# The eighth quad of batch 3's first MLP product as seven half-size products, with a new order at both ends of its chains

## The chip, the cores and the metric

One core of a Trainium2 chip. The metric is the device time of one execution in microseconds (us): the median over runs, lower is better. The kernel before takes 297.79 us (three runs, 297.66 to 298.02). The engines are named as in the profile: PE is TensorE (matmuls; PEld its weight loads), DVE is VectorE, ACT is ScalarE, POOL is GpSimd, SP is SyncE, which here only starts transfers.

## The reference

Block-sparse attention over 4 batches of 768 tokens, then a residual MLP block:

```
attn = softmax(where(mask, q @ k.T / 8, -1e9)) ; x = (attn @ v)      # 4 x 768 x 512
a1 = alpha1 * x + beta1
u  = x + lam * (w_tok @ a1)                                          # over tokens
a2 = alpha2 * u + beta2
h  = maximum(a2 @ w_ch1, 0)                                          # 512 -> 2048
out = u + lam * (h @ w_ch2)                                          # 2048 -> 512
```

The change touches only the last batch (number 3): its first MLP product `a2 @ w_ch1` and the order in which the second, `h @ w_ch2`, begins.

## The kernel before

**Order.** The kernel is emitted by hand-written strings of tokens: each letter takes the next job from a queue, and each engine works its own instructions strictly in the order of emission. `WEAVE` joins the strings; the last four, `W3`, drive the end of batch 3 when no other batch has work left. In them `f` is a job of the first MLP product, `g` one of the second, `S` a VectorE subtraction that prepares the second, `W` and `D` VectorE sums of weights and of activations that prepare the first. The other letters belong to earlier work.

**First stage.** The hidden layer has 2048 rows in 16 blocks of 128; the 768 tokens are two halves c = 0, 1 of 384. Blocks n and n + 8 (`HN` is 8) at both halves form *quad n*: four results of 128 x 384 each. Directly a quad takes four matmuls for each result, 16 in all, each 128 x 128 weights against 384 columns (`job_f1`, matmul at L920, relu by ScalarE at L927). Quads 0 to 6 (`FS` is 7) are computed instead as a 2 x 2 block product with seven half-size products (Strassen's scheme in Winograd's form), two matmuls each, 14 in all (`job_m`, matmul at L1028). Their operands include sums of weight blocks (`job_w`, L978, tile `wsum`) and of activation blocks (`job_d`, L993). Quad 7 was direct.

Within a quad the products 1, 6, 5, 3 accumulate in one bank of the PSUM memory, in this order. After 1, 6 and 5 ScalarE copies the partial sum out (`keep_sum`, L1003, tile `part`), and the next product of the chain may only write once that copy has been read; after 3 ScalarE's relu (L1039) writes the first result. Product 2 has a bank of its own, products 7 and 4 share another; VectorE adds the kept sums to them (L1044) and a relu follows one addition later (`relu_late`, L1011). Product 4 accumulates on the bank of 7 after 7's addition has read it. `last_f1` interleaves the quads: product m of quad n stands in slot 7 n + k, with k = 0, 4, 6, 8, 10, 12, 16 for m = 1, 6, 2, 5, 7, 3, 4. The four direct results of quad 7 stand in slots 1 and 5 (beginning) and 49 and 55 (end).

**Banks.** PSUM gives two `sp` tiles (chains of quads with n % 3 below 2, and chains of the second stage), three `mm` tiles (products 2 and 7, and the like of the second stage) and one `op` tile (chains of quads with n % 3 = 2). A new tile waits until the one that had its place has been read.

**Second stage.** The same scheme: for a pair of token tiles t and t + 3 (t = 0, 1, 2) seven products of eight matmuls with 256 columns each (`job_p` calls `mul`, matmul at L1184), whose results VectorE adds to `x_sb` (`plus`, L1194). Product 1 of tile t needs the first eight hidden blocks at c = 0, so the results of (n,3) for all quads. VectorE forms four differences a tile first (`job_s`, L1157: S1 writes X1, S2 X2, S3 and S4 overwrite parts of `hts`); product 6 needs X2, 7 needs S3, 5 X1, 3 S4. They can be done in halves: `R1` for quads 0 to 3, `R2` for 4 to 7, `ALL` for both. `P_ORDER` and `S_ORDER` hold the order of products and differences. Finished rows are stored by SP and, at the very end, by ScalarE's queue (`emit_store`, L1083).

Of the kernel before, what the change touches and what calls it, by code (L numbers as in the profile page):

```python
# [18 lines left out]
B = 4  # L19
H = 8  # L20
S = 768
D = 64
# [3 lines left out]
DM = 512  # L26
P = 128
# [53 lines left out]
]  # L81
W3 = [
# [4 lines left out]
]  # L87
STR = (2, 3)
HN = NH // 2
HC = DM // 2  # L90
FS = 7
FW = 6
WEAVE = W1 + W2 + W2L + W3
ENG = {
    "kT0": 0,
# [154 lines left out]
def kernel(  # L250
# [211 lines left out]
    def sp_tile():  # L462
        return psum.tile([P, 2, 512], FP, name="sp", tag="sp", bufs=2)
# [6 lines left out]
    def mm_tile(shape=(P, DM), dt=FP):  # L470
        return psum.tile(list(shape), dt, name="mm", tag="mm", bufs=3)

    def op_tile(shape):
        phase["op"] += 1
        if phase["first"] and phase["op"] % 2 == 0:
            return mm_tile(shape)
        return psum.tile(shape, FP, name="op", tag="op", bufs=1)
# [246 lines left out]
    rest = ptile([P, P], FP, "rest")  # L724
# [225 lines left out]
        7: (3, 3),  # L950
    }

    def w_of(name, ks, n):
        if isinstance(name, int):
            at = n.start // FW
            return wsum[at][:, name - 1, ks, (n.start - FW * at) * P : (n.stop - FW * at) * P]
        r, c = int(name[0]) - 1, int(name[1]) - 1
        at = slice((HN * r + n.start) * P, (HN * r + n.stop) * P)
        return w1b[:, 2 * c + ks.start : 2 * c + ks.stop, at]
# [6 lines left out]
        return uTs[B - 1][:, 2 * r + ks.start : 2 * r + ks.stop, ts(1 - c, QC)]  # L966

    def job_w(n, ks, cs):
        at = cs.start // FW
        if len(wsum) == at:  # L970
            tag, bufs = (("x_sb", 3), ("xs", 4))[at]
            shape = [P, 4, 2, (cs.stop - cs.start) * P]
            wsum.append(ap_.tile(shape, BF, name="wsum", tag=tag, bufs=bufs))
        a, b, op = WSUM[n]
        for name in (a, b):
            for k in range(ks.start, ks.stop):
                assert isinstance(name, str) or ("W", name, k, at) in did
        nc.vector.tensor_tensor(  # L978
            out=w_of(n, ks, cs), in0=w_of(a, ks, cs), in1=w_of(b, ks, cs), op=op
        )  # L980
        did.update(("W", n, k, at) for k in range(ks.start, ks.stop))
# [32 lines left out]
    def job_m(n, m):  # L1014
        b = B - 1
        if m == 1 and n % 3 < 2:
            chain[(n, 1)] = sp_tile()[:, 0]
        elif m == 1:
            chain[(n, 1)] = op_tile([P, DM])[:]
        elif m in (2, 7):  # L1020
            chain[(n, m)] = mm_tile()[:]
        ps = chain[(n, {2: 2, 7: 7, 4: 7}.get(m, 1))]
        w, u = PROD1[m]
        for k in range(2):
            ks = slice(k, k + 1)
            assert isinstance(w, str) or ("W", w, k, n // FW) in did
            assert isinstance(u, str) or ("D", u, k) in did
            nc.tensor.matmul(  # L1028
                ps[:, 0:QC],
                w_of(w, ks, slice(n, n + 1))[:, 0],  # L1030
                u_of(u, ks)[:, 0],
                start=(m in (1, 2, 7) and k == 0),
                stop=(k == 1),
                skip_group_check=True,
            )
        if m in (1, 6, 5):
            keep_sum(n, m)
        elif m == 3:
            nc.scalar.activation(h_row(b, 0, n), ps[:, 0:QC], AF.Relu)  # L1039
            did.add(("f", b, 0, n))  # L1040
        else:
            part, c, row = {2: (1, 1, n), 7: (5, 0, HN + n), 4: (6, 1, HN + n)}[m]
            h = h_row(b, c, row)
            nc.vector.tensor_tensor(  # L1044
                out=h, in0=ps[:, 0:QC], in1=chain[(n, "s", part)][:], op=ALU.add
            )
            relu_late()
            raw.append((h, ("f", b, c, row)))

    def last_f1():  # L1050
        at = {1: 0, 6: 4, 2: 6, 5: 8, 7: 10, 3: 12, 4: 16}
        slot = {7 * n + k: (n, m) for n in range(FS) for m, k in at.items()}
        rest = [(c, r + n) for c in range(2) for n in range(FS, HN) for r in (0, HN)]
        jobs = []
        for k in range(max(slot) + 1):
            if k in slot:
                jobs.append(slot[k])
            elif rest and k in (1, 5, 49, 55):
                jobs.append((B - 1,) + rest.pop(0))
        return jobs + [(B - 1,) + j for j in rest]  # L1060

    chs = {}

# [106 lines left out]
    }  # L1170
    banks = {}

    def mul(b, t, n, ps, start, cols=slice(0, HC)):
        a, m, need = PROD[n]
        assert m in bq or all((m, r) in did for r in range(0, HN, 2))
        if need:
            assert all(("S", b, t, need, r) in did for r in range(HN))
        c, half = {"1": (0, 0), "X": (1, 0)}.get(a[0], (1, 0))
        if need == 0:
            h, half = divmod(int(a) - 11, 10)  # L1180
            assert all(("f", b, h, HN * half + r) in did for r in range(HN))
        rows = [r for r in range(HN) if r != FS - 1] + [FS - 1]
        for r in rows:
            nc.tensor.matmul(  # L1184
                ps,
                a_of(b, t, a)[:, r],
                b_rows(m, r)[:, 0, cols],
                start=(start and r == rows[0]),
                stop=(r == rows[-1]),
                skip_group_check=True,  # L1190
            )

# [5 lines left out]

    lo, hi = slice(0, HC), slice(HC, DM)

    def job_p(b, t, n):
        x = x_sbs[b]
        last = (b, t) == (B - 1, NT // 2 - 1)
        bk = banks.setdefault((b, t), {})
        if n in (1, 2, 7):
            bk[n] = sp_tile()[:, 0] if n == 1 else mm_tile()[:]
        if n == 3 and not last and 2 not in bk:
            bk[2] = mm_tile()[:]
        if n == 1:
            mul(b, t, 1, bk[1][:, lo], True)  # L1210
            plus(x[:, t, lo], bk[1][:, lo])
        elif n == 2:
            mul(b, t, 2, bk[2][:, lo], True)
            if last or b < B - 1:
                plus(x[:, t, lo], bk.pop(2)[:, lo])
            if last:
                emit_store(b, t, lo)
        elif n == 6:
            mul(b, t, 6, bk[1][:, lo], False)
            plus(x[:, t + 3, lo], bk[1][:, lo])  # L1220
        elif n == 7:
            mul(b, t, 7, bk[7][:, lo], True)
            plus(x[:, t + 3, hi], bk[7][:, lo])
        elif n == 5:
            mul(b, t, 5, bk[1][:, lo], False)
            plus(x[:, t : t + 4 : 3, hi], twice(bk[1][:, lo]))
        elif n == 4:
            mul(b, t, 4, bk[7][:, lo], False)
            plus(x[:, t + 3, lo], bk[7][:, lo])
            emit_store(b, t + 3, slice(0, DM))  # L1230
        elif last:
            for h in range(2):
                sl = slice(HC + h * P, HC + h * P + P)
                ps = (mm_tile(), op_tile([P, DM]))[h]
                mul(b, t, 3, ps[:, sl], True, ts(h, P))
                plus(x[:, t, sl], ps[:, sl])
                emit_store(b, t, sl, (nc.sync, nc.scalar)[h])
        else:
            sl = hi if b < B - 1 else slice(0, DM)
            mul(b, t, 3, bk[2][:, hi], b < B - 1)  # L1240
            plus(x[:, t, sl], bk[2][:, sl])
            emit_store(b, t, slice(0, DM))
        did.add((b, t, n))
# [36 lines left out]
    def start_mlp(b):  # L1280
# [8 lines left out]
        if b not in STR:  # L1289
# [2 lines left out]
            ]  # L1292
            return
        todo["g"] += [
            lambda j=j: job_p(b, *j) if len(j) == 2 else job_f2(b, *j[:2])
            for j in P_ORDER[b]
        ]
        todo["S"] += [lambda t=t, n=n, r=r: job_s(b, t, n, r) for t, n, r in S_ORDER[b]]
# [5 lines left out]
        + [(3, g, "g") for g in range(4)]  # L1304
        + [(t, 1) for t in (1, 2)]
        + [(t, n) for t in (1, 2) for n in REST],
        3: [(t, n) for n in (1, 2) for t in range(2)]
        + [(t, n) for t in range(2) for n in REST]
        + [(2, n) for n in (1, 2) + REST],
    }  # L1310
    ALL, R1, R2 = slice(0, HN), slice(0, HN // 2), slice(HN // 2, HN)
    S_ORDER = {
        2: [(t, n, ALL) for t in (1, 2) for n in (1, 2, 3, 4)],
        3: [(t, n, R1) for t in range(2) for n in (1, 2, 3)]
        + [(t, n, r) for t in range(2) for n, r in ((1, R2), (2, R2), (3, R2), (4, ALL))]
        + [(2, n, ALL) for n in (1, 2, 3, 4)],
    }

    def start_pair(i):
# [155 lines left out]
    def token(t, p):  # L1475
# [34 lines left out]
    both = slice(0, 2)  # L1510
    todo["W"] = [
        lambda n=n, k=k: job_w(n, k, slice(0, FW)) for n in (1, 3, 2, 4) for k in halves
    ] + [lambda n=n: job_w(n, both, slice(FW, FS)) for n in (1, 3, 2, 4)]
    todo["D"] = [lambda: job_d(1, both)] + [
        lambda n=n, k=k: job_d(n, k) for k in halves[::-1] for n in (2, 3, 4)
    ]
# [33 lines left out]
```

## Time and profile before

| | |
|---|---|
| median of three runs | 297.79 us (297.66 to 298.02) |
| profiled execution | 299.3 us, of which the span from first to last instruction 297.6 us |
| TensorE clock granted, mean | 0.999 |
| PE busy | 288.8 us |
| DVE busy | 239.1 us |
| ACT busy | 217.1 us |
| POOL busy | 110.0 us |
| first stage of batch 3 | from 256.58 us to about 276.4 us |
| second stage of batch 3 | from about 275.2 us to 294.1 us |

Times of rows are microseconds from the start of the span. A timeline row gives the start, the stretch covered, the engine, the line of the kernel, the operation, tile written and tiles read, their shapes, and how many instructions were merged (x2); in brackets the idle time ahead and what ended it. A TensorE row's stretch reaches to the modelled end of its last matmul, so consecutive rows overlap, and it is the distance from start to start that tells what a step costs the engine.

### The profile page before, as it was taken

How to read it: one execution, taken by the hardware profiler on the slowest of the kernel's cores; microseconds unless marked ns; L12 is line 12 of the kernel's file. 1: busy time of each engine (PE TensorE's matmuls, PEld its weight loads, DVE VectorE, ACT ScalarE, POOL GpSimd, SP SyncE). 2: the span in 40 equal slices, each digit the busy share in tenths (PEclk: the TensorE clock that was granted, in tenths of full speed). 3: DMA queues.
4: the chain of work that ended last, by engine and by line, in shares of the span. 5: the costliest groups of instructions: out<-in, count | busy, mean ns of one | idle time of the engine just before them, and what ended most of it. 6: DMA issues, size and time to landing. Idle time of an engine off the chain costs nothing.

```text
span 297.6 us, 7560 instructions
## 1 busy us (share of the span) xinstructions
PE 288.8 (97%) x3080; PEld 192.8 (65%) x3099; DVE 239.1 (80%) x492; ACT 217.1 (73%) x324; POOL 110.0 (37%) x149
## 2 busy tenths in 40 slices
PE   7999999999999999999999999999999999999995
PEld 2688878665467565565576566555567679765884
DVE  4988889995678887978768778795946999889994
ACT  5999989999798972999779690989869754577000
POOL 8997878632343720356322350335320300000000
PEclk9999999999999999999999999999999999999999
DMA  6999999971392996628853869743520211400032
GB/s 178 208 195 159 198 143 205 190 134 26 95 141 61 107 192 99 117 66 116 102 121 65 132 97 143 91 119 45 93 62 2 53 37 28 141 1 3 0 140 75
DMA packets 57275, 31.10 MB, mean 105 GB/s; under 512 B 37204, under 2 KB 54016, under 8 KB 57240
## 3 DMA queue, kind: packets, MB, share of 16 engines
q0 software_dynamic: 16752, 14.22, 33.4%
q1 hardware_dynamic: 40020, 15.92, 27.5%
q8 instruction: 24, 0.39, 0.6%
q10 hardware_dynamic: 468, 0.47, 0.5%
q14 instruction: 11, 0.09, 0.1%
HBM read 29.75 MB, written 6.29 MB: 121 GB/s over the span
## 4 chain that ended last, share of the span: by engine, by line
PE 82%; DMA 6%; DVE 6%; ACT 3%; POOL 1%; issue 1%; SPq 0%; POOLq 0%
PE mm L920 21%; PE mm L1070 14%; PE sp L602 8%; PE mm L847 8%; PE op L672 8%; PE mm L1184 5%; PE sp L1184 4%; DMA qpad<-in_q_dram 3%; PE mm L602 3%; PE mm L1028 2%; PE sp L1028 2%; ACT eT L620 2%; DMA uraw<-ubf 2%; PE op L649 2%; DVE eT L637 2%; PE mm L823 1%
## 5 line engine op out<-in xcount | busy, mean ns | idle before, releaser
L620 ACT ACTIVATE eT<-sp,expb 128x1024 f16<-128x1024 f32 x111 | 118.5, 1119 | 2.8 <-PE sp L602 2.2
L637 DVE TENSOR_TENSOR eT<-eT,mask 128x1024 f16<-128x1024 f16 x99 | 80.1, 835 | 14.2 <-ACT eT L620 14.0
L920 PE MATMUL mm<-uT,w1b 128*128 128x384 bf16 x400 | 73.9, 326 | 0.1
L706 POOL TENSOR_TENSOR a1pp<-x_sb,vbc 128x384 bf16<-128x384 f32 x25 | 28.5, 1140 | 120.5 <-DVE x_sb L690 85.9
L620 ACT ACTIVATE eT<-mm,expb 128x512 f16<-128x512 f32 x66 | 41.7, 685 | 26.5 <-PE mm L602 26.2
L927 ACT ACTIVATE hts<-mm 128x384 bf16<-128x384 f32 x100 | 47.1, 502 | 11.8 <-PE mm L920 11.1
L920 PEld LDWEIGHTS <-w1b 128*128 128x128 bf16 x400 | 37.2, 98 | 25.0 <-issue 2.6
L1070 PE MATMUL mm<-w2b,hts 128*128 128x512 bf16 x205 | 52.2, 379 | 0.9 <-issue 0.2
L672 PEld LDWEIGHTS <-eT 128*128 128x128 f16 x792 | 29.8, 98 | 9.2 <-issue 1.7
L1070 PEld LDWEIGHTS <-hts 128*128 128x128 bf16 x224 | 19.8, 98 | 22.3 <-issue 3.9
L672 PE MATMUL op<-vext,eT 128*128 128x65 f16 x792 | 32.1, 194 | 0.8 <-DVE x_sb L690 0.7
L602 PE MATMUL sp<-qTs,kTs 88*128 88x512 bf16 (+1 forms) x120 | 26.9, 325 | 1.4 <-ACT eT L620 0.7
L707 POOL TENSOR_TENSOR a1pp<-a1pp,vbc 128x384 bf16<-128x384 bf16 x25 | 26.7, 1070 | 2.0
L847 PE MATMUL mm<-a1pp,wtokT 128*128 128x256 bf16 x216 | 25.9, 273 | 0.1
L847 PEld LDWEIGHTS <-wtokT 128*128 128x128 bf16 x216 | 20.6, 98 | 5.6 <-issue 1.8
L1184 PEld LDWEIGHTS <-hts 128*128 128x128 bf16 x208 | 19.6, 98 | 3.0 <-issue 0.3
L859 DVE TENSOR_TENSOR x_sb<-x_sb,mm 128x512 f32<-128x512 f32 x18 | 12.3, 685 | 9.9 <-PE mm L847 9.8
L602 PE MATMUL sp<-qhT,khT 64*128 64x256 bf16 (+1 forms) x176 | 19.8, 322 | 0.0
L602 PEld LDWEIGHTS <-khT 64*128 64x128 bf16 x264 | 10.6, 94 | 12.7 <-issue 9.2
L649 PEld LDWEIGHTS <-eT 128*128 128x128 f16 x360 | 14.9, 97 | 3.8 <-issue 0.3
L1079 DVE TENSOR_TENSOR x_sb<-x_sb,mm 128x512 f32<-128x512 f32 x14 | 9.6, 685 | 8.8 <-PE mm L1070 6.7
L690 DVE TENSOR_TENSOR x_sb<-op,rcp 128x384 f32<-128x384 f32 x28 | 15.6, 557 | 1.0
(135 smaller groups left out, 384.9 us busy)
## 6 DMA issues: line engine op xcount, KB each, us to landing
out_dram<-x_sb SPq DMA_DIRECT2D x23, 256.0 KB
qpad<-in_q_dram POOLq DMA_DIRECT2D x15, 192.0 KB, 4.4
kr<-in_k_dram POOLq DMA_DIRECT2D x15, 192.0 KB, 5.4
vr<-in_v_dram POOLq DMA_DIRECT2D x15, 192.0 KB, 6.9
w1b<-in_moe_w_ch_dram POOLq DMA_DIRECT2D x4, 512.0 KB, 9.0
w2b<-in_moe_w_ch_dram POOLq DMA_DIRECT2D x4, 512.0 KB, 8.4
hts<-in_moe_w_tok_dram POOLq DMA_DIRECT2D x2, 576.0 KB, 8.3
x_sb<-in_k_dram ACTq DMA_DIRECT2D x2, 192.0 KB
```

The source lines that it names most:

```text
L602: nc.tensor.matmul(sp[jj][:, dst], lhsT, rhs, start=True, stop=True, skip_group_check=True,)
L620: nc.scalar.activation(dst, at, AF.Exp, bias=expb[:], scale=SCALE)
L637: nc.vector.tensor_mul(out=e, in0=e, in1=keep)
L649: nc.tensor.matmul(op[0][:, o, :], ets[u][:, jj, h * QB + n * P : h * QB + n * P + P], vexts[i % NVB][:, w, 2 * jp + jj, :], start=op[1] == 0,
L672: nc.tensor.matmul(op[0][:, o, :], ets[u][:, jj, h * QB + n * P : h * QB + n * P + P], vexts[i % NVB][:, w, 2 * jp + jj, :], start=op[1] == 0,
L706: eng.tensor_tensor(out=dst, in0=x_sbs[b][:, :, cols], in1=bc[0], op=ALU.mult)
L707: eng.tensor_tensor(out=dst, in0=dst, in1=bc[1], op=ALU.add)
L847: nc.tensor.matmul(ps[:, o], wtokT[:, os_, ts(2 * n + o, P)], a1pps[i][:, os_, :], start=(os_ == 0 and o == 0), stop=(os_ == NT - 1 and o ...
L920: nc.tensor.matmul(ps[:, 0:QC], w1b[:, dk, ts(n, P)], uTs[b][:, dk, ts(c, QC)], start=(dk == 0), stop=(dk == 3),)
L927: nc.scalar.activation(h_row(b, c, n), ps[:, 0:QC], AF.Relu)
L1070: nc.tensor.matmul(ps[:], ht[:, nk, ts(o % 3, P)], w2b[:, nk, :], start=(nk == 0), stop=(nk == NH - 1),)
L1184: nc.tensor.matmul(ps, a_of(b, t, a)[:, r], b_rows(m, r)[:, 0, cols], start=(start and r == rows[0]), stop=(r == rows[-1]), skip_group_che ...
```

## The change

Quad 7 goes the way of the others: `FS` and the direct slots disappear, and `job_m` covers all eight quads. Four weight sums for quad 7 are added (tile `wsum` of one block each for quads 6 and 7); the eight such sums no longer stand at the end of the first string of `W3`, but between the first `f` jobs. The list `FIRST` spells out the first twenty slots of the first stage; the later ones keep their pattern, four slots earlier. (n,m) below is product m of quad n. The first stage begins with (0,1), (0,2), (1,1), (1,2), (0,6), (2,1), (1,6), (2,2), (0,5), (0,7), (1,5), (1,7), (0,3), (2,6), (1,3), (0,4).

At its end the second stage's product 1 of tile 0 is cut into four pieces of two hidden blocks each, in the `op` tile instead of an `sp` tile. The end of the first stage reads, with 0-1 for product 1 of tile 0: (7,1), (6,5), (5,4), (6,7), (7,6), (6,3), (7,2), first piece of 0-1, (7,5), (6,4), (7,7), second piece, (7,3), third piece, 1-1, (7,4), fourth piece, 2-1, 0-2, 1-2, 0-6, and so on. Product 2-1 used to come after 1-3. Of the differences, only those of tile 0 are still made in halves, and of these only S1 and S2; all others are made whole, 14 instructions where there were 18.

```diff
 W3 = [
-    "a p p p g s g g T S T S T S S S d g g U g v g D g D D g D g D g D D W W W W",
-    "f f f f f f f f f f f f f f f f f f f f f",
-    "f f f f f f f f f f f f f f f f f S f f f S f f f f S f f S f f f S S f f",
-    "g f S S g g S g S g S g S g S g S g g S g S g S g g g g S g g g g g",
+    "a p p p g s g g T S T S T S S S d g g U g v g D g D D g D g D g D D",
+    "f f f W W f W W f f f f f W f f f f f W f f f f f f f W f f",
+    "W f f f f f f f f f f f f f f f S f f f f S f f f f f f f f f g f f f g f g g f",
+    "g S S g g S g S g S g S g S g S g g S g S g S g g g S g g g g g",
 ]
...
-FS = 7
 FW = 6
+FIRST = [
+    (0, 1), (0, 2), (1, 1), (1, 2), (0, 6), (2, 1), (1, 6), (2, 2), (0, 5), (0, 7),
+    (1, 5), (1, 7), (0, 3), (2, 6), (1, 3), (0, 4), None, None, None, (1, 4),
+]
...
+    w0 = [0] + list(range(FW, HN))
+
+    def w_at(n):
+        return max(0, n - FW + 1)
...
     def last_f1():
-        at = {1: 0, 6: 4, 2: 6, 5: 8, 7: 10, 3: 12, 4: 16}
-        slot = {7 * n + k: (n, m) for n in range(FS) for m, k in at.items()}
-        rest = [(c, r + n) for c in range(2) for n in range(FS, HN) for r in (0, HN)]
-        jobs = []
-        for k in range(max(slot) + 1):
-            if k in slot:
-                jobs.append(slot[k])
-            elif rest and k in (1, 5, 49, 55):
-                jobs.append((B - 1,) + rest.pop(0))
-        return jobs + [(B - 1,) + j for j in rest]
+        slot = {k: nm for k, nm in enumerate(FIRST) if nm}
+        for n in range(2, HN):
+            for m, k in {1: 0, 6: 4, 2: 6, 5: 8, 7: 10, 3: 12, 4: 16}.items():
+                if (n, m) not in FIRST:
+                    assert 7 * n + k - 4 not in slot
+                    slot[7 * n + k - 4] = (n, m)
+        return [slot[k] for k in sorted(slot)]
...
-    def mul(b, t, n, ps, start, cols=slice(0, HC)):
+    def mul(b, t, n, ps, start, cols=slice(0, HC), rows=slice(0, HN)):
...
-        rows = [r for r in range(HN) if r != FS - 1] + [FS - 1]
-        for r in rows:
+        for r in range(rows.start, rows.stop):
...
         if n in (1, 2, 7):
-            bk[n] = sp_tile()[:, 0] if n == 1 else mm_tile()[:]
+            if n in bk:
+                pass
+            elif n != 1:
+                bk[n] = mm_tile()[:]
+            elif (b, t) == (B - 1, 0):
+                bk[n] = op_tile([P, DM])[:]
+            else:
+                bk[n] = sp_tile()[:, 0]
...
         if n == 1:
-            mul(b, t, 1, bk[1][:, lo], True)
+            mul(b, t, 1, bk[1][:, lo], True, rows=rows)
+            if rows.stop < HN:
+                return
             plus(x[:, t, lo], bk[1][:, lo])
...
-        3: [(t, n) for n in (1, 2) for t in range(2)]
+        3: [(0, 1, slice(r, r + 2)) for r in (0, 2, 4)]
+        + [(1, 1), (0, 1, slice(6, HN)), (2, 1)]
+        + [(t, 2) for t in range(2)]
         + [(t, n) for t in range(2) for n in REST]
-        + [(2, n) for n in (1, 2) + REST],
+        + [(2, n) for n in (2,) + REST],
...
-        3: [(t, n, R1) for t in range(2) for n in (1, 2, 3)]
-        + [(t, n, r) for t in range(2) for n, r in ((1, R2), (2, R2), (3, R2), (4, ALL))]
-        + [(2, n, ALL) for n in (1, 2, 3, 4)],
+        3: [(0, n, r) for r in (R1, R2) for n in (1, 2)]
+        + [(0, n, ALL) for n in (3, 4)]
+        + [(t, n, ALL) for t in (1, 2) for n in (1, 2, 3, 4)],
...
-    ] + [lambda n=n: job_w(n, both, slice(FW, FS)) for n in (1, 3, 2, 4)]
+    ] + [
+        lambda n=n, c=c: job_w(n, both, slice(c, c + 1))
+        for c in range(FW, HN)
+        for n in (1, 3, 2, 4)
+    ]
```

More of the change, by code (lines that the diff above doesn't have):

```diff
@@ L951 @@
     }
+    w0 = [0] + list(range(FW, HN))
+    def w_at(n):
+        return max(0, n - FW + 1)
     def w_of(name, ks, n):
         if isinstance(name, int):
-            at = n.start // FW
-            return wsum[at][:, name - 1, ks, (n.start - FW * at) * P : (n.stop - FW * at) * P]
+            at = w_at(n.start)
+            return wsum[at][:, name - 1, ks, (n.start - w0[at]) * P : (n.stop - w0[at]) * P]
         r, c = int(name[0]) - 1, int(name[1]) - 1
@@ L968, in job_w @@
     def job_w(n, ks, cs):
-        at = cs.start // FW
+        at = w_at(cs.start)
         if len(wsum) == at:
-            tag, bufs = (("x_sb", 3), ("xs", 4))[at]
+            tag, bufs = ("xs", 4) if at else ("x_sb", 3)
             shape = [P, 4, 2, (cs.stop - cs.start) * P]
@@ L1025, in job_m @@
             ks = slice(k, k + 1)
-            assert isinstance(w, str) or ("W", w, k, n // FW) in did
+            assert isinstance(w, str) or ("W", w, k, w_at(n)) in did
             assert isinstance(u, str) or ("D", u, k) in did
@@ L1177, in mul @@
             assert all(("S", b, t, need, r) in did for r in range(HN))
+        ends = (0, HN - 1)
         c, half = {"1": (0, 0), "X": (1, 0)}.get(a[0], (1, 0))
@@ L1180, in mul @@
             h, half = divmod(int(a) - 11, 10)
-            assert all(("f", b, h, HN * half + r) in did for r in range(HN))
-        rows = [r for r in range(HN) if r != FS - 1] + [FS - 1]
-        for r in rows:
+            assert all(("f", b, h, HN * half + r) in did for r in range(rows.start, rows.stop))
+        for r in range(rows.start, rows.stop):
             nc.tensor.matmul(
@@ L1187, in mul @@
                 b_rows(m, r)[:, 0, cols],
-                start=(start and r == rows[0]),
-                stop=(r == rows[-1]),
+                start=(start and r == ends[0]),
+                stop=(r == ends[1]),
                 skip_group_check=True,
@@ L1199, with job_p @@
     lo, hi = slice(0, HC), slice(HC, DM)
-    def job_p(b, t, n):
+    def job_p(b, t, n, rows=slice(0, HN)):
         x = x_sbs[b]
@@ L1294, in start_mlp @@
         todo["g"] += [
-            lambda j=j: job_p(b, *j) if len(j) == 2 else job_f2(b, *j[:2])
+            lambda j=j: job_f2(b, *j[:2]) if j[-1] == "g" else job_p(b, *j)
             for j in P_ORDER[b]
```

## The prediction

> **What bounds the kernel now.** I read the page first, then the busy time by stretches of the end, then the end's three engines in order of time.
>
> ```profile
> span 297.6 us, 7560 instructions
> PE 288.8 (97%) x3080; PEld 192.8 (65%) x3099; DVE 239.1 (80%) x492; ACT 217.1 (73%) x324; POOL 110.0 (37%) x149
> ...
> PEclk9999999999999999999999999999999999999999
> ```
>
> ```profile
> 262.30:272.20 9.90, 9.90 (x63) 5.97 (x61) 9.12 (x28) 7.29 (x18) 0.00 (x0) 1.00 0.01 2
> ...
> 275.20:282.50 7.30, 7.30 (x68) 6.43 (x66) 6.74 (x19) 0.55 (x2) 0.00 (x0) 1.00 0.00 0
> ```
>
> TensorE works without a break at full clock; after each stretch stand PE, PEld, DVE, ACT and POOL busy time. VectorE (DVE) is not far behind. A busy PE also covers short waits, since a matmul's record outlasts the issue of the next, so I read the steps from start to start (TensorE in order of time):
>
> ```profile
> 256.58 0.49 PE L1028 MATMUL sp<-uT,w1b 128*128 128x384 bf16 x2
> 256.90 0.81 PE L920 MATMUL mm<-uT,w1b 128*128 128x384 bf16 x4
> 257.63 0.48 PE L1028 MATMUL sp<-uT,wsum 128*128 128x384 bf16 x2
> ...
> 259.58 0.49 PE L1028 MATMUL mm<-uT,wsum 128*128 128x384 bf16 x2
> 259.98 0.86 PE L1028 MATMUL sp<-uT,wsum 128*128 128x384 bf16 x4
> 260.69 0.49 PE L1028 MATMUL mm<-uT,w1b 128*128 128x384 bf16 x2
> ...
> 262.31 0.49 PE L1028 MATMUL op<-uT,wsum 128*128 128x384 bf16 x2
> 262.63 0.49 PE L1028 MATMUL sp<-uT,wsum 128*128 128x384 bf16 x2
> ...
> 272.06 0.49 PE L1028 MATMUL mm<-uT,w1b 128*128 128x384 bf16 x2
> 272.49 0.81 PE L920 MATMUL mm<-uT,w1b 128*128 128x384 bf16 x4
> ...
> 273.46 0.49 PE L1028 MATMUL mm<-uT,w1b 128*128 128x384 bf16 x2
> 273.88 0.48 PE L1028 MATMUL mm<-uT,wsum 128*128 128x384 bf16 x2
> 274.25 0.48 PE L1028 MATMUL sp<-uT,wsum 128*128 128x384 bf16 x2
> ...
> 286.02 1.04 PE L1184 MATMUL mm<-kTs,hts 128*128 128x256 bf16 x8
> 286.90 1.04 PE L1184 MATMUL mm<-w2b,hts 128*128 128x256 bf16 x8
> ```
>
> A product of two matmuls takes 0.325 us of TensorE (262.31 to 262.63, and 272.06 would be followed at 272.385), four matmuls 0.65, a second-stage product of eight 0.873 (286.02 to 286.90, to the hundredth). What a step is longer than that is a wait: 0.08 at 257.63 (256.90 + 0.65 = 257.55), 0.075 at 259.98, 0.06 inside the group at 259.98 (it should end at 260.63), 0.105 at 272.49, 0.095 at 273.88, 0.045 at 274.25. Together **0.46 us of waits**, all in the first 4 and the last 3 us of the first stage; no later step is longer.
>
> **The change, part by part.** (n,m) is product m of quad n in the first stage; t-m is product m of token tile t in the second.
>
> *Two matmuls fewer.* The direct eighth quad is 4 x 4 matmuls (the four L920 groups), as seven products it is 7 x 2. 16 - 14 = 2, and 0.325 us a pair: **-0.325 us** straight off TensorE's stream. The Trainium skill, page "TensorE: Matmul & The Clock Gate", section "Back-to-back issue gap", gives warm N/2.4 + 2.5 ns for an isolated matmul, 162.5 ns at 384 columns, which the step here repeats; but for a sustained stream it gives about 131 ns at 512 columns, by which the pair would be worth at most 0.26 and the forecast about 0.06 us later. The trace decides for 0.325.
>
> *The old waits.* A link of a chain is TensorE to ScalarE to TensorE:
>
> ```profile
> 257.10 0.48 ACT L1003 COPY part<-sp 128x384 f32<-128x384 f32 x1 [0.98 <-PE sp L1028]
> ...
> 273.33 0.49 ACT L927 ACTIVATE hts<-mm 128x384 bf16<-128x384 f32 x1 [0.53 <-PE mm L920]
> 273.72 0.47 ACT L1003 COPY part<-sp 128x384 f32<-128x384 f32 x1
> ```
>
> (0,1) starts at 256.58, its records end at 257.07, the copy runs 257.10 to 257.58, (0,6) starts at 257.63: 1.05 us a link. The old order left 0.975 between the first links of quads 0 and 1, so both waited 0.08. FIRST puts four products, 1.30 us, between (0,1) and (0,6), and four between (1,1) and (1,6). The waits at 273.88 and 274.25 come from a direct product: its relu at 273.33 ends at 273.82, which frees the bank that 273.88 takes, and pushes the copy to 273.72, which ends at 274.19. That at 272.49 is a bank too, freed by an addition of VectorE (second of these rows: two additions, the first ends at 272.45):
>
> ```profile
> 262.19 0.56 DVE L1044 TENSOR_TENSOR hts<-mm,part 128x384 bf16<-128x384 f32 x1 [0.25 <-PE mm L1028]
> 262.66 0.25 DVE L1011 TENSOR_SCALAR hts<-hts 128x384 bf16<-128x384 bf16 x1
> 262.82 0.55 DVE L1044 TENSOR_TENSOR hts<-mm,part 128x384 bf16<-128x384 f32 x1
> ...
> 271.89 1.01 DVE L1044 TENSOR_TENSOR hts<-mm,part 128x384 bf16<-128x384 f32 x2
> ```
>
> Direct products are gone, so I count all of it: **-0.46 us** (bounds: 0 if each wait comes back elsewhere, -0.46).
>
> *The eighth chain.* (7,1), (7,6), (7,5), (7,3) need 1.05 us a link. The new order leaves 4 products (1.30), then 3 products and a quarter of 0-1 (0.975 + 0.218 = 1.19), then the same again. The three early quarters are moved work, not added: **0**, with 0.14 us of slack in the last two links. Without that cover each would cost 0.08.
>
> *VectorE in the head.* Eight small weight sums now stand between the additions instead of four ahead of them.
>
> ```profile
> 257.65 0.49 DVE L978 TENSOR_TENSOR wsum<-w1b 128x256 bf16<-128x256 bf16 x2
> 258.06 0.28 DVE L978 TENSOR_TENSOR wsum<-wsum,w1b 128x256 bf16<-128x256 bf16 x1
> ```
>
> At 0.2 (257.65 to 258.06 for two) to 0.29 us each, I take 0.24, the four new ones and the eighth quad's three additions and relus (0.47 and 0.16, from 262.19 to 262.66 to 262.82) add about 2.8 us to VectorE. First to be missed is (0,4), which accumulates on the bank that (0,7)'s addition reads. Counting the queue: (0,2)'s addition takes the place of the first sum at 257.65, two sums follow, to 258.6; then addition, relu, two sums, addition, relu, one sum take 0.47 + 0.16 + 0.48 + 0.47 + 0.16 + 0.24, so (0,7)'s addition starts at about 260.6 and ends 261.2, and (0,4) is due as the sixteenth product at 256.58 + 15 x 0.325 = 261.45. **0**, slack 0.2. Everything on TensorE stands behind (0,4), so lateness beyond 0.2 is paid in full.
>
> *The turn to the second stage.* All 56 products (18.20) and 0-1, 1-1, 2-1, 0-2, 1-2 (4.37) come before 0-6, which starts at 279.15. It needs X2 of tile 0. (7,4) is issued at 275.98 and read from 276.50; then addition 0.47, relu, the addition of 0-1, relu and two half subtractions that wait for each other:
>
> ```profile
> 277.44 0.26 DVE L1011 TENSOR_SCALAR hts<-hts 128x384 bf16<-128x384 bf16 x1
> 277.80 0.43 DVE L1157 TENSOR_TENSOR xs<-hts 128x512 bf16<-128x512 bf16 x1
> 278.26 0.42 DVE L1157 TENSOR_TENSOR xs<-xs,hts 128x512 bf16<-128x512 bf16 x1
> ```
>
> 276.50 + 0.47 + 0.16 + 0.33 + 0.36 + 0.46 + 0.42 = 278.7. **0**, slack 0.4.
>
> *VectorE in the second stage.* Tile 1's subtractions are no longer half done in the first stage; three of 0.34 become 0.60, at a place where the queue has no idle left:
>
> ```profile
> 284.48 0.42 DVE L1194 TENSOR_TENSOR x_sb<-x_sb,sp 128x256 f32<-128x256 f32 x1
> 284.81 0.69 DVE L1157 TENSOR_TENSOR xs<-hts 128x1024 bf16<-128x1024 bf16 x1
> 285.42 0.41 DVE L1194 TENSOR_TENSOR x_sb<-x_sb,mm 128x256 f32<-128x256 f32 x1
> 285.75 0.68 DVE L1157 TENSOR_TENSOR xs<-xs,hts 128x1024 bf16<-128x1024 bf16 x1
> 286.35 0.68 DVE L1194 TENSOR_TENSOR x_sb<-x_sb,sp 128x512 f32<-128x512 f32 x1
> ```
>
> A narrow addition steps 0.335, a full subtraction 0.60, and so I count a wide addition, which lasts the same 0.68. 0-6's addition starts at 280.22 (279.15 + 1.04 + 0.03). Up to the addition of 1-6 stand three narrow and two wide additions and four subtractions: 3 x 0.335 + 6 x 0.60 = 4.6, so that one runs 284.82 to 285.25. 1-5, due at 279.15 + 7 x 0.873 = 285.26, needs it and starts 0.03 late. 1-7's addition, 0.335 + 0.60 later, ends at 286.18; 1-4, due 286.17, starts 0.06 late. With 3 ns more a step, as the rows have it in places: **+0.12 us** (bounds 0 and, at the worst step below, 1.7). Later ones wait less: the last tile has no subtractions of another behind it.
>
> *One cover less.* 2-1 moved ahead, so 2-2 now follows 1-3 at once. If its bank were the one that 1-3's addition frees, TensorE would stand about 1 us.
>
> ```profile
> 287.97 0.69 DVE L1194 TENSOR_TENSOR x_sb<-x_sb,mm 128x512 f32<-128x512 f32 x1
> ...
> 288.64 1.04 PE L1184 MATMUL mm<-w2b,hts 128*128 128x256 bf16 x8
> ```
>
> The addition ends at 288.66 and 2-2 began at 288.64: another bank, **0**. What follows the last product, one addition and its store, is unchanged.
>
> Sum: -0.325 - 0.46 + 0.12 = **-0.67 us**. The profiled execution took 299.3 (span 297.6 and 1.7 around it), so 298.63; the median of the runs, 297.79, lies 1.5 below that one and 0.2 above its span, and the same difference gives **297.12**.
>
> **The rivals.** *Waits only move.* The head and the end are new orders with slacks of 0.14 to 0.2 us; if waits like the old ones appear there, only the two matmuls are won: 297.79 - 0.325 = **297.47**. For it: six such waits existed; against it: each old one has a cause that goes.
> *VectorE late in the head.* If the seven steps ahead of (0,7)'s addition take 0.11 more each, as dependent ones do (below), (0,4) starts 0.77 - 0.2 = 0.55 late: **297.67**. Against it: these are not dependent on one another.
> *VectorE bounds the second stage: slower.* From 0-6's addition to 1-7's stand 11 instructions without slack, so each hundredth on a step costs TensorE 0.11. Where one depends on the one ahead, its step is longer:
>
> ```profile
> 236.22 0.68 DVE L1157 TENSOR_TENSOR xs<-hts 128x1024 bf16<-128x1024 bf16 x1
> 236.93 0.69 DVE L1157 TENSOR_TENSOR xs<-xs,hts 128x1024 bf16<-128x1024 bf16 x1
> ```
>
> 0.71 for 0.60. At 0.11 more on all 11: 1.2, and 8 more instructions up to 2-6's addition, 0.88 less the 0.37 that 2-5 has to spare: 1.7 in all, **298.82**. It decides from about 0.055 a step, where it eats the 0.67. Against it: in the rows from 284.48 on the two kinds alternate, are independent, and start before the end of the one ahead. The Trainium skill, page "VectorE: DVE Perf Modes", section "The DRAIN you can't avoid", says that the next operation does not start until the pipe is empty; taken strictly that is this rival. The row at 285.42, 0.08 before the end of the one at 284.81, speaks against taking it so.
>
> **How the numbers follow.** Forecast 0.58, waits only move 0.22, late in the head 0.10, VectorE bound 0.10. A difference of 0.2%, 0.6 us, is about what a measurement tells from none. The forecast is only just over it (bounds -0.79 with no new wait, 297.00, to about -0.5 with 0.3 of new waits, 297.3), so a little of its chance goes to the same side: faster 0.55, within 0.2% 0.36, slower 0.09 (the last rival, short of its mild cases). The range takes in the two middle rivals and leaves out the slow one: 296.85 to 297.8.
>
> **What would show it.** Right: 112 matmuls of 384 columns after the turn, 0.325 apart throughout with 0-6 at about 22.57 us behind (0,1); waits of TensorE only ahead of 1-5 and 1-4, under 0.15 in all; no idle time of VectorE from 0-6's addition to 1-7's. Wrong: a step above 0.325 before (0,4) or along quad 7; (2,2)'s start held to the end of 1-3's addition; steps of VectorE near 0.71 in the second stage.

## The result and the profile after

| | before | after |
|---|---|---|
| median, 15 runs each | 298.00 us | 297.22 us |
| ratio, 95% interval | | 0.9971 [0.9959, 0.9984] |
| ratio of a second series, 12 and 29 runs | | 0.9983 [0.9974, 0.9992] |
| profiled execution | 299.3 us, span 297.6 | 297.57 us, span 295.9 |
| first matmul of the first stage, from the span's start | 256.58 us | 255.44 us |
| from there to the start of the kernel's last matmul ("the stretch" below) | 37.27 us | 36.68 us |
| waits of TensorE in the stretch | 0.46 us | 0.18 us |

The kernel became faster by 0.8 us by the medians. The profiled executions differ by 1.7 us in span, and 1.14 of it had passed before the first instruction that the change moves. That part belongs to the executions, not to the change: a kernel whose program up to there is that of before ("direct head" below) came to the first stage at 255.06 us. What the change does is read in the stretch, where single records fit to the hundredth: **-0.59 us**, 0.20% of the kernel, inside both intervals.

TensorE after, in order of time (start, stretch covered, engine, line, operation, tile written and read, shape, count):

```profile
255.44 0.49 PE L1036 MATMUL sp<-uT,w1b 128*128 128x384 bf16 x2
255.77 0.49 PE L1036 MATMUL mm<-uT,w1b 128*128 128x384 bf16 x2
...
256.42 0.49 PE L1036 MATMUL mm<-uT,w1b 128*128 128x384 bf16 x2
256.74 0.49 PE L1036 MATMUL sp<-uT,wsum 128*128 128x384 bf16 x2
...
260.32 0.49 PE L1036 MATMUL mm<-uT,w1b 128*128 128x384 bf16 x2
...
270.72 0.49 PE L1036 MATMUL mm<-uT,wsum 128*128 128x384 bf16 x2
271.04 0.90 PE L1036 MATMUL sp<-uT,wsum 128*128 128x384 bf16 x4
271.78 0.49 PE L1036 MATMUL mm<-uT,w1b 128*128 128x384 bf16 x2
272.10 0.38 PE L1189 MATMUL op<-w2b,hts 128*128 128x256 bf16 x2
272.32 0.49 PE L1036 MATMUL sp<-uT,wsum 128*128 128x384 bf16 x2
...
273.51 0.49 PE L1036 MATMUL sp<-uT,wsum 128*128 128x384 bf16 x2
...
278.10 0.60 PE L1189 MATMUL op<-qTs,xs 128*128 128x256 bf16 x4
...
283.33 0.82 PE L1189 MATMUL mm<-qk,hts 128*128 128x256 bf16 x6
...
284.24 1.03 PE L1189 MATMUL sp<-qTs,xs 128*128 128x256 bf16 x8
285.17 1.03 PE L1189 MATMUL mm<-kTs,hts 128*128 128x256 bf16 x8
286.04 1.91 PE L1189 MATMUL mm<-w2b,hts 128*128 128x256 bf16 x16
```

The beginning is dense: (0,6) at 256.74 is the fifth product, 4 x 0.325 behind (0,1), and (0,4) at 260.32 the sixteenth, 15 x 0.325 behind it. At the end of the first stage the first quarter of 0-1 stands at 272.10 and (7,3) at 273.51. Three steps are too long. The four matmuls from 271.04, (7,6) and (6,3), take 0.74 to the next row instead of 0.65: 0.09 before (6,3). 1-7 at 283.33 should be followed by 1-5 at 284.20, and 1-5 at 284.24 by 1-4 at 285.11: 0.03 and 0.06. 1-3 and 2-2 run through in one row at 286.04, so 2-2 has another bank than the one that 1-3's addition frees.

VectorE after: the addition of (0,7), the second half subtraction of tile 0, then from the addition of 0-6 on, then up to that of 1-7:

```profile
259.38 0.55 DVE L1052 TENSOR_TENSOR hts<-mm,part 128x384 bf16<-128x384 f32 x1
...
277.25 0.42 DVE L1162 TENSOR_TENSOR xs<-xs,hts 128x512 bf16<-128x512 bf16 x1
...
279.17 0.42 DVE L1199 TENSOR_TENSOR x_sb<-x_sb,op 128x256 f32<-128x256 f32 x1
279.51 0.69 DVE L1162 TENSOR_TENSOR xs<-hts 128x1024 bf16<-128x1024 bf16 x1
280.11 0.41 DVE L1199 TENSOR_TENSOR x_sb<-x_sb,mm 128x256 f32<-128x256 f32 x1
...
283.18 0.68 DVE L1199 TENSOR_TENSOR x_sb<-x_sb,mm 128x512 f32<-128x512 f32 x1
283.77 0.41 DVE L1199 TENSOR_TENSOR x_sb<-x_sb,sp 128x256 f32<-128x256 f32 x1
284.11 0.68 DVE L1162 TENSOR_TENSOR xs<-hts 128x1024 bf16<-128x1024 bf16 x1
284.71 0.41 DVE L1199 TENSOR_TENSOR x_sb<-x_sb,mm 128x256 f32<-128x256 f32 x1
```

From 279.17 on no row, and none between those shown, has an idle time in brackets. 1-6's addition runs 283.77 to 284.18 and 1-5 starts at 284.24; 1-7's runs 284.71 to 285.12 and 1-4 starts at 285.17. These are the waits of 0.03 and 0.06.

ScalarE after, around the wait before (6,3):

```profile
269.67 0.50 ACT L1047 ACTIVATE hts<-op 128x384 bf16<-128x384 f32 x1
270.31 1.09 ACT L1011 COPY part<-sp 128x384 f32<-128x384 f32 x2
271.57 0.48 ACT L1011 COPY part<-sp 128x384 f32<-128x384 f32 x1 [0.16 <-PE sp L1036]
```

The two copies at 270.31, of (7,1) and (6,5), span 1.09 us; such a pair spans 0.86 elsewhere (270.48 of "ScalarE shifted" below). By the single records the second starts at 270.93 and ends at 271.41, and (6,3) starts at 271.46. That copy is late by 0.24 us (a pair steps 0.38, these two 0.62), and no other engine holds it: (6,5) had left TensorE by 270.6.

### The profile page after: what moved, and what is told of

The parts are those of the page before. It is cut to its first block, busy times and chain, and to the rows that moved or that the text cites. A ratio compares the mean times of both kernels' runs of the same rounds, so it can differ in the third digit from the quotient of the medians.

```text
span 295.9 us, 7583 instructions
## 1 busy us (share of the span) xinstructions
PE 289.2 (98%) x3097; PEld 192.7 (65%) x3097; DVE 240.6 (81%) x498; ACT 217.0 (73%) x324; POOL 110.1 (37%) x149
## 4 chain that ended last, share of the span: by engine, by line
PE 84%; DVE 5%; ACT 4%; DMA 4%; issue 1%; POOL 1%; POOLq 0%
PE mm L923 20%; PE mm L1075 16%; PE sp L605 8%; PE op L675 8%; PE mm L850 8%; PE mm L1189 5%; ACT eT L623 4%; PE mm L605 3%; DMA kr<-in_k_dram 3%; PE sp L1189 3%; PE sp L1036 3%; PE mm L1036 3%; PE op L652 2%; PE mm L826 2%; DVE eT L640 1%; DMA x_sb<-in_q_dram 1%
## 5 line engine op out<-in xcount | busy, mean ns | idle before, releaser
L923 PE MATMUL mm<-uT,w1b 128*128 128x384 bf16 x384 | 70.6, 326 | 0.1
L1075 PE MATMUL mm<-w2b,hts 128*128 128x512 bf16 x224 | 54.7, 380 | 0.0
L930 ACT ACTIVATE hts<-mm 128x384 bf16<-128x384 f32 x96 | 45.1, 501 | 10.1 <-PE mm L923 9.5
L923 PEld LDWEIGHTS <-w1b 128*128 128x128 bf16 x384 | 35.6, 98 | 23.9 <-issue 2.4
```

The lines of the kernel that those rows point to most:

```text
L923: nc.tensor.matmul(ps[:, 0:QC], w1b[:, dk, ts(n, P)], uTs[b][:, dk, ts(c, QC)], start=(dk == 0), stop=(dk == 3),)
L930: nc.scalar.activation(h_row(b, c, n), ps[:, 0:QC], AF.Relu)
L1075: nc.tensor.matmul(ps[:], ht[:, nk, ts(o % 3, P)], w2b[:, nk, :], start=(nk == 0), stop=(nk == NH - 1),)
```

## The experiments

Each kernel below was profiled and timed. "Waits" and "stretch" come from single records as in the table above. Ratios are against runs of the kernel before, in the same series. Dots in an edit stand for lines left out, most of them the strings of tokens, put in step with the new order.

| kernel | matmuls of 384 columns | waits, us | stretch, us | ratio, 95% interval |
|---|---|---|---|---|
| before | 114 | 0.46 | 37.27 | |
| changed | 112 | 0.18 | 36.68 | 0.9971 [0.9959, 0.9984] |
| changed, again | 112 | 0.19 | 36.68 | 0.9983 [0.9974, 0.9992] |
| quad only | 112 | 2.00 | 38.48 | 1.004 [1.0028, 1.0052] |
| no pieces | 112 | 1.00 | 37.49 | 1.0005 [0.9996, 1.0014] |
| old head | 112 | 1.18 | 37.66 | 1.0013 [1.0004, 1.0022] |
| sums first | 112 | 1.43 | 37.92 | 1.0018 [1.0007, 1.0029] |
| late halves | 112 | 0.39 | 36.89 | 0.9986 [0.9977, 0.9996] |
| early halves | 112 | 0.09 | 36.59 | 0.9972 [0.9962, 0.9983] |
| direct head | 114 | 0.24 | 37.06 | 0.999 [0.998, 0.9999] |
| ScalarE shifted | 112 | 0.09 | 36.59 | 0.9974 [0.9964, 0.9984] |
| (6,3) later | 112 | 0.00 | 36.50 | 0.9967 [0.9955, 0.9979] |

**Changed, again.** No edit.

> The changed kernel once more, unaltered. In its first trace the stretch from the first matmul of the first stage to the last matmul of the kernel lasted 36.68 us against 37.27 before, with three waits of TensorE: 0.09 before (6,3), 0.03 before 1-5, 0.06 before 1-4. Theory (the waits at 1-5 and 1-4 follow from VectorE's queue): those two come back within 0.02 us. For the wait before (6,3), which follows from no queue that I counted: if the order of work makes it, it comes back at the same place; if it is an accident of that execution, it is gone and the stretch lasts 36.59. Time 0.2 to 0.3% under the kernel before.

All three waits came back at their places, 0.089, 0.034 and 0.063 us, and the stretch was 36.68. So the wait before (6,3) is made by this program, not by one execution.

**Quad only.** The eighth quad as seven products without the two layouts: slots as of old, 0-1 whole behind the first stage.

```diff
...
-        slot = {k: nm for k, nm in enumerate(FIRST) if nm}
-        for n in range(2, HN):
+        slot = {}
+        for n in range(HN):
...
+                slot[7 * n + k] = (n, m)
...
-        3: [(0, 1, slice(r, r + 2)) for r in (0, 2, 4)]
-        + [(1, 1), (0, 1, slice(6, HN)), (2, 1)]
+        3: [(t, 1) for t in range(3)]
```

> The eighth quad as seven products, with the old pattern of slots at the beginning (nothing stands where the direct results stood) and 0-1 whole behind (7,4). Theory (a chain needs 1.05 us a link, and TensorE stands for what the order leaves open): (0,1) and (0,6) now adjoin, so 0.72 us there and 0.07 each at two further links; at the end 0.07 before (7,5) and (7,3), and 0.71 before (7,4), which waits for (7,7)'s addition. In all about 1.7 us more than the changed kernel, so about 1.1 us (0.4%) slower than the kernel before, though two matmuls fewer. Rival (two matmuls fewer are what counts, the order only shifts waits): 0.1% faster than before or the same.

TensorE of this kernel, its beginning and its end:

```profile
255.19 0.49 PE L1036 MATMUL sp<-uT,w1b 128*128 128x384 bf16 x2
256.24 0.48 PE L1036 MATMUL sp<-uT,wsum 128*128 128x384 bf16 x2 [0.57 <-ACT part L1011]
...
273.91 0.48 PE L1036 MATMUL sp<-uT,wsum 128*128 128x384 bf16 x2
274.95 0.48 PE L1036 MATMUL mm<-uT,w1b 128*128 128x384 bf16 x2 [0.56 <-DVE hts L1052]
```

(0,6) starts 1.05 us after (0,1), the bare length of a link; and (7,4) 1.04 after (7,3), of which 0.72 is a wait for (7,7)'s addition. The stretch is 1.80 longer than the changed kernel's, where 1.7 was expected, and the kernel is 0.4% slower than before: two matmuls fewer save 0.325 us, but without something for TensorE to do inside the links its waits grow by 1.54.

**No pieces** (0-1 whole at the end, new head) and **old head** (old slots, pieces kept) undo one layout each, with the two halves of the edit above.

> The changed kernel with 0-1 whole, and all of the second stage behind (7,4). Theory: (7,5) and (7,3) each wait 0.07 us, and (7,4), now straight behind (7,3), waits 0.7 us for (7,7)'s addition; the stretch is 0.86 longer than the changed kernel's, 37.5 us. Rival (the quarters only change the place of work, since the other chains fill the end): no wait above 0.1, 36.7 us.

> The changed kernel with the old pattern of slots at the beginning, nothing in the place of the direct results. Theory: waits of 0.72 before (0,6) and 0.07 before (0,5) and (0,3), none at the end but those of the changed kernel; the stretch is 0.87 longer, 37.5 us. Rival (ScalarE's copies overlap enough, the beginning costs only the 0.22 of before): 36.9 us.

No pieces: 37.49, with 0.08 before (7,3), 0.715 before (7,4) and 0.10 before (6,3); the one expected before (7,5) did not come, since the late (6,3) had pushed (7,5) back by itself. Old head: 0.73 before (0,6), 0.134 before (0,5) where 0.07 was expected (the link from (0,6) lasts 1.11 us by the single records, not 1.05), 0.08 before (0,3), and 0.13 in two waits before (7,6) and (6,3), where the late copy of ScalarE is that of (7,1) and the next one stands behind it: 37.66 for 37.5. Each layout is worth 0.8 to 1.0 us, either alone leaves the kernel no faster than before, and both are needed for a gain.

**Sums first.** The eight weight sums ahead of the first addition.

```diff
-    "a p p p g s g g T S T S T S S S d g g U g v g D g D D g D g D g D D",
-    "f f f W W f W W f f f f f W f f f f f W f f f f f f f W f f",
+    "a p p p g s g g T S T S T S S S d g g U g v g D g D D g D g D g D D W W W W W W W W",
+    "f f f f f f f f f f f f f f f f f f f f f f f",
...
```

> The changed kernel with all eight weight sums ahead of the first product's addition, as the four stood before. Theory (VectorE has about 0.2 us to spare in the beginning): the additions of (0,2) and its followers come 0.7 to 0.9 us later, (0,7), which takes the bank that (0,2)'s addition frees, waits about 0.73 us, and the stretch from the first matmul of the first stage to the last lasts about 37.4 us against 36.68. Rival (VectorE has room in the beginning, as its first additions wait for copies anyway): 36.7 us, no wait there.

TensorE, then ScalarE, of this kernel:

```profile
257.70 0.49 PE L1036 MATMUL sp<-uT,wsum 128*128 128x384 bf16 x2
258.65 0.48 PE L1036 MATMUL mm<-uT,wsum 128*128 128x384 bf16 x2 [0.46 <-DVE hts L1052]
259.60 0.48 PE L1036 MATMUL sp<-uT,wsum 128*128 128x384 bf16 x2 [0.46 <-ACT part L1011]
```

```profile
256.98 0.48 ACT L1011 COPY part<-sp 128x384 f32<-128x384 f32 x1 [0.23 <-PE sp L1036]
258.69 0.48 ACT L1011 COPY part<-op 128x384 f32<-128x384 f32 x1 [1.23 <-DVE hts L1052]
259.06 0.87 ACT L1011 COPY part<-sp 128x384 f32<-128x384 f32 x2
```

There are two waits of 0.62 us, not one of 0.73. (0,7) waits for the bank, as expected. The second was missed: the kept sum of (2,1) needs one of the two places for kept sums of product 1, which (0,2)'s late addition frees; ScalarE stands 1.23 us before that copy, and the copy of (1,6) is queued behind it, for which (1,5) waits at 259.60. An engine that works in order hands one late release to everything behind it.

**Late halves.** Tile 1's first three differences in two halves each, at the same place: three more instructions on VectorE.

```diff
...
-        + [(t, n, ALL) for t in (1, 2) for n in (1, 2, 3, 4)],
+        + [(1, n, r) for n in (1, 2, 3) for r in (R1, R2)]
+        + [(1, 4, ALL)]
+        + [(2, n, ALL) for n in (1, 2, 3, 4)],
```

> The changed kernel with tile 1's first three differences cut in two at the place where they stand: three more instructions on VectorE, about 0.07 us each, all between 0-6's addition and 1-6's. Theory (no slack there): 1-5 waits about 0.24 us instead of 0.03, 1-4 0.06 as before, the stretch is 0.2 longer, 36.9 us. Rival (the waits at 1-5 and 1-4 come from banks or from TensorE's own order, not from VectorE's length): both stay as they were, 36.7 us.

TensorE of this kernel, 1-7, 1-5 and 1-4:

```profile
283.56 0.38 PE L1189 MATMUL mm<-tmore,hts 128*128 128x256 bf16 x2
284.02 1.03 PE L1189 MATMUL sp<-qTs,xs 128*128 128x256 bf16 x8
284.95 1.03 PE L1189 MATMUL mm<-kTs,hts 128*128 128x256 bf16 x8
```

The last two matmuls of 1-7 at 283.56 should be followed at 283.78; 1-5 waits 0.24 us. The stretch grew by 0.21, three times 0.07. VectorE has no slack there: of what was added to it TensorE paid the whole.

**Early halves.** The first halves between the last products of the first stage.

```diff
...
-        3: [(0, n, r) for r in (R1, R2) for n in (1, 2)]
+        3: [(t, n, R1) for t, n in ((0, 1), (0, 2), (1, 1), (1, 2), (1, 3))]
+        + [(0, n, R2) for n in (1, 2)]
         + [(0, n, ALL) for n in (3, 4)]
-        + [(t, n, ALL) for t in (1, 2) for n in (1, 2, 3, 4)],
+        + [(1, n, R2) for n in (1, 2, 3)]
+        + [(1, 4, ALL)]
+        + [(2, n, ALL) for n in (1, 2, 3, 4)],
```

> The changed kernel with the first halves of tile 1's first three differences made between the last products of the first stage, where VectorE has idle time, and the second halves at the old place. Theory: no wait before 1-5 and 1-4, none new at the end of the first stage; the stretch is 0.09 shorter than the changed kernel's (36.59, or 36.50 without the wait before (6,3)). Rival (the end of the first stage has no more room on VectorE than the second): a wait of 0.1 to 0.3 before (7,4) or 0-6, 36.7 to 36.9 us.

TensorE of this kernel, the end of 1-7, 1-5 and 1-4:

```profile
283.80 0.38 PE L1189 MATMUL mm<-tmore,hts 128*128 128x256 bf16 x2
284.02 1.04 PE L1189 MATMUL sp<-qTs,xs 128*128 128x256 bf16 x8
284.89 1.04 PE L1189 MATMUL mm<-kTs,hts 128*128 128x256 bf16 x8
```

The steps are 0.22 and 0.87, those of two and eight matmuls. 36.59: both waits of the second stage are gone and none came instead.

**Direct head.** The kernel before, with only the first fifteen jobs in another order.

```diff
-        return jobs + [(B - 1,) + j for j in rest]
+        first = [
+            (0, 1), (B - 1, 0, 7), (1, 1), (B - 1, 0, 15), (0, 6), (0, 2), (1, 6), (1, 2),
+            (0, 5), (2, 1), (0, 7), (1, 5), (0, 3), (1, 7), (0, 4),
+        ]
+        jobs += [(B - 1,) + j for j in rest]
+        return first + [j for j in jobs if j not in first]
```

> The kernel before, eighth quad direct, with only the beginning of the first stage put in another order: the two direct results stand so that every link of the first chains has 1.05 us or more. Theory: the waits before (0,6), (1,6) and (0,3) go (0.22 us), those at the end stay (0.10, 0.09, 0.04); the stretch lasts 37.06 us against 37.27, so about a third of the changed kernel's gain needs no eighth quad. Rival (the direct results themselves make those waits): 37.27.

TensorE of this kernel, (0,1) and (0,6):

```profile
255.06 0.49 PE L1028 MATMUL sp<-uT,w1b 128*128 128x384 bf16 x2
...
257.01 0.49 PE L1028 MATMUL sp<-uT,wsum 128*128 128x384 bf16 x2
```

Between them lie 1.95 us, six pairs of matmuls without a wait. The stretch is 37.06: the three waits of the head are gone, and the three at the end have their old lengths, 0.104, 0.091 and 0.044 us. A third of the gain was to be had without the eighth quad. The time agrees (0.999), though its interval nearly reaches 1.

**ScalarE shifted** and **(6,3) later** start from early halves and ask for the cause of the late copy.

```diff
+    spare = ptile([P, 1], FP, "spare")
...
+            for _ in range(12):
+                nc.scalar.copy(spare[:], expb[:])
```

> The kernel with early halves, and twelve tiny copies (128x1) more on ScalarE, into a tile that nothing reads, at a place where ScalarE has 5 us idle, before the first stage. The order of the work after it is the same, only ScalarE's instructions stand twelve places later in its program. The wait of 0.089 us before (6,3) comes from the copy of (6,5), which starts 0.34 us after the wait ahead of it is over, where such copies elsewhere start 0.10 after; an 8 KB transfer of instructions starts 0.6 us later in each trace. Theory A (the place in ScalarE's program makes it late, as where a new piece of the program is begun): the copy of (6,5) starts 0.10 after, the wait before (6,3) is gone, the stretch lasts 36.50 us instead of 36.59, and some ScalarE instruction twelve places earlier, the copy of (4,5) or a neighbour, is late. Theory B (the order of work makes it, two chains in sp tiles side by side): nothing changes, 36.59.

ScalarE of this kernel, then TensorE:

```profile
265.84 0.48 ACT L1012 COPY part<-op 128x384 f32<-128x384 f32 x1
266.46 0.48 ACT L1012 COPY part<-sp 128x384 f32<-128x384 f32 x1
...
270.48 0.86 ACT L1012 COPY part<-sp 128x384 f32<-128x384 f32 x2
```

```profile
266.57 0.49 PE L1037 MATMUL op<-uT,wsum 128*128 128x384 bf16 x2
266.99 0.48 PE L1037 MATMUL sp<-uT,wsum 128*128 128x384 bf16 x2
```

The pair of (7,1) and (6,5) at 270.48 now spans 0.86. The copy of (4,5) at 266.46, twelve places earlier in ScalarE's order, is the late one: it starts 0.62 after the copy ahead, where a pair steps 0.38. (4,3) at 266.99 pays, 0.09 us. The transfer of 8 KB of instructions that stood at 271.6 in the changed kernel and at 271.4 with early halves is found at 267.1; this row is from the view of transfers between 266.9 and 267.5 us (queue, packets, MB, share):

```profile
q14 instruction: 1, 0.01, 5.1%
```

So theory B falls, and of theory A the place in ScalarE's program is shown; that a new piece of the program begins there is not. The number 36.50 did not come, since the late copy met another link with as little to spare.

```diff
-        return [slot[k] for k in sorted(slot)]
+        jobs = [slot[k] for k in sorted(slot)]
+        i, j = jobs.index((6, 3)), jobs.index((7, 2))
+        jobs[i], jobs[j] = jobs[j], jobs[i]
+        return jobs
```

> The kernel with early halves, with (6,3) and (7,2) exchanged in the order of the first stage, so that (6,3) comes 0.325 us later. Theory (only the distance from (6,5) to (6,3) counts, whatever makes the copy late): no wait before (6,3), none elsewhere, stretch 36.50 us; time about 0.3% under the kernel before. Rival (the lateness of ScalarE is handed on to the copy of (7,6), and so to (7,5)): a wait of up to 0.1 before (7,5), 36.6 us.

TensorE of this kernel from (6,7) and (7,6) on, then ScalarE's copies of (7,1) and (6,5):

```profile
270.18 0.49 PE L1036 MATMUL mm<-uT,wsum 128*128 128x384 bf16 x2
270.50 0.49 PE L1036 MATMUL sp<-uT,wsum 128*128 128x384 bf16 x2
270.82 0.49 PE L1036 MATMUL mm<-uT,w1b 128*128 128x384 bf16 x2
271.15 0.49 PE L1036 MATMUL sp<-uT,wsum 128*128 128x384 bf16 x2
271.48 0.38 PE L1192 MATMUL op<-w2b,hts 128*128 128x256 bf16 x2
```

```profile
269.77 1.09 ACT L1011 COPY part<-sp 128x384 f32<-128x384 f32 x2
```

0.325 throughout: TensorE has no wait left in the stretch, 36.50 us, the fastest of all these kernels at 0.9967 [0.9955, 0.9979], 296.99 us median. The copy of (6,5) is as late as before (the pair spans 1.09 us again); it only meets more distance.

## Why the prediction was right, point by point

- **Two matmuls fewer, -0.325.** Right. Direct head has 114 matmuls and 0.24 of waits, (6,3) later 112 and none: 37.06 - 0.24 - 36.50 = 0.32 us.
- **The old waits, -0.46.** All six are gone. For the head the cause was as read: the rule of 1.05 us a link gave the new waits of quad only and old head within 0.01 us at (0,6) and (0,3), though a link of 1.11 showed at (0,5), and direct head removed the three waits of the head by order alone. For the three at the end the cause (the row of VectorE meant for 272.49 is the last of its group, at 271.89) is read from rows only; they stay in direct head and go with the whole change, and no run takes them apart. The step also counted the bound at which none comes back, and one did: before (6,3), 0.09 us, from a late copy on ScalarE that no counted queue contains. It is the one term that the forecast lacked. By it two of the signs named ahead were missed: the waits are 0.18 and not under 0.15, and 0-6 starts 22.66 behind (0,1) instead of 22.57.
- **The eighth chain, 0.** Right: no wait at (7,6), (7,5), (7,3) or (7,4). Its price without cover was put at 0.08 a link. No pieces shows the larger price that the step did not name: with 1-1 gone from between (7,3) and (7,4), (7,4) waits 0.72 for an addition.
- **VectorE in the head, 0 with 0.2 to spare.** Right in the changed kernel, with 0.39 to spare: (0,7)'s addition ran 259.38 to 259.93, and (0,4) started when due, at 260.32. Sums first shows what would have been missed first: not (0,4), but (0,7)'s bank and ScalarE's place for a kept sum, both hanging on (0,2)'s addition.
- **The turn, 0 with 0.4 to spare.** X2 was complete at 277.67 (the second half subtraction starts 277.25 and lasts 0.42), 0-6 started at 278.10: 0.43.
- **VectorE in the second stage, +0.12.** Right in place and mechanism; the size was 0.09, which the steps without the 3 ns of allowance had given (0.03 and 0.06). Late halves and early halves moved it by 0.21 up and 0.09 down.
- **The sum** was -0.67, the stretch shows -0.59: 0.09 more at (6,3), 0.03 less in the second stage, and 0.02 that stays within rounding.
- **The rivals.** "Waits only move" came true for one wait of 0.09. VectorE was not late in the head. VectorE did bound the second stage, but at steps of 0.60 (279.51 to 280.11) and not 0.71: the strict reading of the Trainium skill's page "VectorE: DVE Perf Modes", section "The DRAIN you can't avoid", would give the slow rival, and these rows, each started about 0.08 before the end of the one ahead, do not agree with it. They do agree with what that section adds, that a next operation which is not held starts earlier.

The median fell by 0.78 in the first series and 0.46 in the second, for 0.59 in the stretch. Both intervals hold 0.9980, so nothing beyond the stretch is needed, and nothing beyond it is shown. That the median of 297.22 lies so close to the forecast of 297.12 is in part luck: the forecast set out from 297.79, where the kernel before now measured 298.00, and the median fell by 0.19 more than the stretch. And whether the gain passes the line of 0.2% that the forecast drew is not settled: 0.29% in the first series, 0.17% in the second.

## What to carry to other kernels

When independent chains share one engine, write down the length of a link (here matmul, copy, hand-over: 1.05 us, at one place 1.11) and count what the order puts inside each; a cheaper algorithm without that cover loses more than it saves, as quad only did. At beginnings and ends, where the other chains are missing, independent work cut to size is what fills the links. And before lengthening instructions on a helper engine, add up its queue over the stretch: with no idle time left, the main engine pays. Here three times 0.07 us on VectorE became 0.21 on TensorE.

## What the runs showed of the hardware

One ScalarE copy starts 0.24 us late at a fixed place of ScalarE's program. Counted in ScalarE's records it has the same number in all ten traces of kernels with the eighth quad as products; in quad only and old head, where two more instructions stand ahead, that number falls on the copy of (7,1) instead of (6,5). Twelve more instructions ahead of it moved the lateness to the copy twelve places earlier in the work, and an 8 KB transfer of instructions moved with it: it starts 0.65 us behind the late copy in the changed kernel (270.93 and 271.58) and with ScalarE shifted (266.46 and 267.12). So among these kernels the place in the program, not the data or the order of the work, makes the copy late.

What it is at that place stays open. The transfer starts only after the late copy has begun, so the copy did not wait for that transfer to land; the two are not tied to the hundredth either, for in (6,3) later the distance is 0.94 (270.38 and 271.32). In the kernel before such a transfer starts at 272.03, and no copy near it is late. The Trainium skill, page "Runtime: NRT & Kernel Launch", section "Instruction fetch mechanics", says that engines are refilled in blocks of 16 KiB and that crossing a boundary is mostly hidden; the transfer in these traces has 8 KB, and if the fetch is the cause, 0.24 us of it was not hidden, of which TensorE paid 0.09. That it is the fetch itself that delays the copy is inferred from the two moving together, not seen.
